# The M blocks of a feed-forward stage in the free columns of its two product banks, with a new order of that stage

## The chip, the cores and the metric

The kernel runs on one core of a Trainium2 chip. Its time is the device time of one execution in microseconds (us). TensorE (PE in the profile; PEld is its weight load), VectorE (DVE), ScalarE (ACT), GpSimd (POOL) and SyncE (SP, which issues the DMAs here) each work through a queue of their own in order, and wait for each other through semaphores.

## The reference, cut to what matters

```python
def reference(q, k, v, phi, w1, w2, w_in, w_out):
    x = attention(q, k, v)           # 4 x 8 heads, 576 positions, windowed -> 2304 x 512
    logits = x @ phi                 # 32 slots
    d = softmax over tokens (logits)
    slot_input = d.T @ x             # 32 x 512, four slots for each of 8 experts
    for e in range(8):
        slot_out[e] = relu(slot_input[e] @ w1[e]) @ w2[e]
    c = softmax over slots (logits)
    x = c @ slot_out                 # 2304 x 512
    h = x @ w_in                     # the feed-forward stage: 2304 x 2048
    return (relu(h) ** 2) @ w_out    # 2304 x 512
```

## The kernel before, in words

Attention, slots and experts come first, up to about 159 us. The change is in the last stage, the feed-forward.

The stage doesn't build `x`. Since x @ w_in = c @ (slot_out @ w_in), it first makes M = slot_out @ w_in, 32 rows, in ten **M blocks** `M0` to `M9` (four of 128 columns, six of 256; `CHUNKS`), each as soon as its weights are there. A block has three parts (`m_ops`): `M4.0` is the product on TensorE into a tile `pm` in PSUM, `M4.1` a rounded copy of it into `M3` in SBUF (tile `M`, on ACT or DVE), `M4.2` the rest of the rounding, taken as a difference by DVE (L953), which reads `pm` too. The other operand is `C3`, the transposed `c`, rounded and split in the same way: eight blocks of it are transposed by TensorE into tiles `c3p` (token `cp`), copied by ACT (`ca`) and finished by DVE (`cv`). Blocks 0 to 3 are the first half `C3a`, 4 to 7 the second `C3b`.

Then 96 **steps** follow. A step is one group of 384 tokens and one block of 128 hidden columns: `h` is the product of `C3` and `M3` into a PSUM tile `ph`, `u` its relu by ACT, `q` the rounded square (tile `hi`, on ACT or DVE), `g` the exact square, `l` their difference (tile `lo`, DVE), `oa` six matmuls of 512 columns with `hi` into the sums `acc`, `ob` three more with `lo`. `e` takes a finished sum out of `acc`.

The weights come as 64-bit floats and are converted on the chip: tokens `i4.0` to `i4.4` for block 4 of w_in, `o4.0` to `o4.4` for w_out (`.0` and `.1` on ACT or DVE, `.2` to `.4` on DVE), and `s4.0`, `s4.1` split w_out into two rounded tiles `wohl`. `.4` frees the slot of a ring of five, and the next load goes there.

What sets the order is the table `SEQ`: every token is one operation, and each engine gets its own in the order of the table. `SEGS` says which token groups (pairs of 384) run through which hidden blocks after each other: pair 0 with blocks 0 to 3, pair 1 with all 16, pair 0 with the rest, pair 2 with all. A pair that is left unfinished is parked in SBUF (`part`, `slotD`) and added back later.

Of the eight PSUM banks, six hold `acc`, and two are a pool `h` with two buffers, from which `ph`, `pm` and, from the fifth block on, `c3p` take a buffer in the order in which they are asked for. A buffer comes free when all readers of its tile have run.

Of the kernel before, what the change touches and what calls it, by code (L numbers as in the profile page):

```python
# [67 lines left out]
i4.3V i5.0A oa u o4.2V u ob q.V g.A q.V g.A h oa l u o5.1A l q.V ob g.V o5.0A i4.4V h oa e.A e.A e.V u ob l i6.1A q.V
h oa e.V e.A e.V g.A u ob o4.3V q.A h oa g.A l u l q.A g.V ob o6.1A o4.4V h oa u l s4.0A q.V ob g.V s4.1V h oa u q.A l
g.A i5.2V ob l h oa i5.3V u i7.1A q.V ob g.A i5.4V h oa u l q.A g.V ob o5.2V l M4.0 o5.3V oa M4.1A i6.0V M4.2V o6.0A  # L70
ob o5.4V h o7.1A h oa i6.2V u s5.0V u ob q.V g.A q.A g.V h oa u l l q.A g.A s5.1V ob h oa l u i6.3V i8.1A ob q.A g.V
M5.0 i6.4V oa l M5.1A o6.2V i7.0A M5.2V ob o6.3V o7.0A h h oa i7.2V u u o6.4V q.A ob g.A h q.V g.A oa l s6.0A l i7.3V
u ob o8.1A h oa s6.1V q.A g.A i7.4V u ob q.A M6.0 g.A l i9.1A l oa o7.2V M6.1A o7.3V i8.0A ob M6.2V oa o8.0A o7.4V h h
i8.2V s7.0A ob i8.3V M7.0 u u q.V g.A h cp q.V g.A oa l M7.1A l u s7.1V ca.A ob q.A g.A h M7.2V oa i9.0A l i8.4V u ob
o9.1A h q.V oa g.A o8.2V u l o9.0A ob q.V g.V h oa o8.3V u q.A g.A l ob o8.4V h oa u l s8.0A q.V ob g.V s8.1V h oa u
q.A l g.A cv ob l M8.0 i9.2V i9.3V oa M8.1A o9.2V ob M8.2V i9.4V cp h h ca.A oa u o9.3V u q.A ob g.A cv q.A g.V h oa l
u l q.A o9.4V g.A ob h l oa s9.0A u s9.1V ob q.A g.A M9.0 l oa M9.1A M9.2V ob h h oa u u q.V g.A q.V g.A ob l l h oa u
q.A g.V l ob h oa u q.A g.V l ob h oa u q.A g.V l ob h oa e.A e.V e.A u ob q.A g.V h l oa e.A e.V e.A u ob q.A g.V h l
oa u q.A g.V l ob h oa u q.A g.V l ob h oa u q.A g.V l ob h oa u q.A g.V l ob h oa u q.A g.V l ob h oa u q.A g.V l ob
h oa u q.A g.V l ob h oa u q.A g.V l ob h oa u q.A g.V l ob h oa u q.A g.V l ob h oa u q.A g.V l ob h oa u q.A g.V l  # L80
ob h oa u q.A g.V l ob h oa u q.A g.V l ob h oa u q.A g.V l ob h oa u q.A g.V l ob h oa u q.A g.V l ob h oa u q.A g.V
l ob h oa u q.A g.V l ob h oa u q.A g.V l ob h oa u q.A g.V l ob h oa u q.A g.V l ob h oa e.V u e.V q.A g.A e.V ob l h
# [1084 lines left out]
```

## Time and profile before

| | us |
|---|---|
| median of 3 runs | 407.81 (407.49 to 410.29) |
| the profiled execution's own time | 407.48 |
| its span, first to last instruction | 405.7 |
| TensorE busy | 388.1 (96%) |
| VectorE busy | 271.4 (67%) |
| ScalarE busy | 250.3 (62%) |
| GpSimd busy | 81.8 (20%) |

The busy times are means over stages with different limits. What a part of the stage is worth is seen where engines stand idle, and in what ends that.

### The profile page before, as it was taken

Reading aid. Unit: us, or ns where it says so; the run is one execution under the profiler, and the core shown is the slowest. Engines: PE = TensorE matmul, PEld = TensorE weight load, DVE = VectorE, ACT = ScalarE, POOL = GpSimd, SP = SyncE. Lnnn points to the kernel's source line nnn. Section 1 sums busy time; section 2 is a strip of 40 time slices with the busy share of each in tenths; the row PEclk is TensorE's granted clock in tenths of the full one; section 3 lists DMA queues with packets and bytes.
Section 4 is the critical chain, followed back from the end, with each engine's and each line's share of the span. In section 5 each row is a group of like instructions: output and inputs, shape, how many; then the busy total and the mean of one; then the engine's idle time right before and its main releaser. Section 6 shows DMA issues by size and latency. Waiting matters only on the chain.

```text
span 405.7 us, 8004 instructions
## 1 busy us (share of the span) xinstructions
PE 388.1 (96%) x2874; PEld 296.9 (73%) x2874; DVE 271.4 (67%) x624; ACT 250.3 (62%) x744; POOL 81.8 (20%) x167
## 2 busy tenths in 40 slices
PE   6899999999999998799999889999999999999996
PEld 3787887888874333578877677788888888888885
DVE  2699888788753227699999989665454565444452
ACT  4588888888853114699778974665444454444442
POOL 2677775757611002000000000000000000000000
PEclk9699999999999999699999999999999999999999
DMA  7998599999989999844454400003000040000004
GB/s 214 415 418 306 166 303 294 319 307 299 320 309 342 389 387 378 331 132 142 145 205 134 180 0 0 2 13 145 0 0 2 0 155 2 1 2 1 0 2 155
DMA packets 31992, 70.11 MB, mean 173 GB/s; under 512 B 2257, under 2 KB 5329, under 8 KB 31953
## 3 DMA queue, kind: packets, MB, share of 16 engines
q1 hardware_dynamic: 31952, 69.61, 48.7%
q8 instruction: 23, 0.38, 0.4%
q14 instruction: 17, 0.13, 0.1%
HBM read 64.88 MB, written 4.72 MB: 172 GB/s over the span
## 4 chain that ended last, share of the span: by engine, by line
PE 71%; DVE 12%; DMA 7%; ACT 5%; issue 3%; SPq 1%; POOL 0%; ACTq 0%; POOLq 0%; DVEq 0%
PE acc L1003 26%; PE acc L1009 13%; PE s L323 6%; PE o L372 5%; DMA slotC<-in_w_dram 4%; PE ph L975 4%; PE pt L358 3%; PE psh L759 3%; PE xnp L409 3%; DVE slotA L842 2%; PE s L320 2%; PE pacc L428 2%; DMA slotC<-in_kq_dram 2%; DVE cv L847 2%; DVE lo L997 2%
## 5 line engine op out<-in xcount | busy, mean ns | idle before, releaser
L1003 PE MATMUL acc<-wohl,hi 128*128 128x512 f32 x580 | 153.8, 398 | 1.0 <-ACT hi L990 1.0
L1003 PEld LDWEIGHTS acc<-wohl,hi 128*128 128x128 f32 x580 | 108.1, 190 | 24.2 <-ACT hi L990 1.6
L982 ACT ACTIVATE u<-ph 128x384 f32<-128x384 f32 x96 | 46.5, 490 | 76.4 <-PE ph L975 74.0
L1009 PE MATMUL acc<-wohl,lo 128*128 128x512 f32 x290 | 85.2, 396 | 0.0
L992 DVE TENSOR_TENSOR g<-u 128x384 f32<-128x384 f32 x66 | 36.9, 558 | 54.9 <-ACT u L982 54.9
L1009 PEld LDWEIGHTS acc<-wohl,lo 128*128 128x128 f32 x290 | 54.8, 189 | 13.0
L997 DVE TENSOR_TENSOR lo<-g,hi 128x384 fp32r<-128x384 f32 x96 | 52.8, 556 | 10.9 <-ACT g L990 3.2
L343 ACT ACTIVATE p<-s,ns 128x96 f32<-128x96 f32 x144 | 47.4, 343 | 6.7 <-DVE ns L337 6.3
L990 ACT ACTIVATE hi<-u 128x384 fp32r<-128x384 f32 x80 | 42.0, 526 | 2.2
L352 POOL TENSOR_TENSOR p<-p,ns 128x288 f32<-128x288 f32 x48 | 32.1, 671 | 27.2 <-DVE ns L351 14.1
L343 ACT ACTIVATION_READ_ACCUMULATOR p<-s,ns 128x1 f32 x144 | 29.7, 206 | 0.0
L337 DVE TENSOR_REDUCE ns<-s 128x3 f32<-128x288 f32 x48 | 21.7, 451 | 10.7 <-PE s L323 10.2
L713 POOL COPY c3n<-c_all 96x96 f32<-96x96 f32 x24 | 6.9, 326 | 101.0 <-PE c3p L725 101.0
L358 PE MATMUL pt<-ident,p 128*96 128x128 f32 x144 | 24.9, 284 | 0.6 <-POOL p L352 0.6
L199 POOL TENSOR_TENSOR slotC<-slotC,zero 32x384 f32<-32x384 f32 (+1 forms) x27 | 20.0, 746 | 7.8 <-ACT qz L312 6.6
L323 PE MATMUL s<-slotC,qz 128*128 128x96 f32 x126 | 18.4, 286 | 2.4 <-DVE qz L310 2.4
L323 PEld LDWEIGHTS s<-slotC,qz 128*128 128x128 f32 x126 | 17.6, 208 | 4.1 <-issue 3.8
L842 DVE SCALAR_TENSOR_TENSOR slotA<-slotA 128x1024 int32<-128x1024 int32 (+1 forms) x18 | 18.9, 1048 | 0.5 <-ACT slotA L835 0.4
L835 ACT ACTIVATE slotA<-slotA 128x1024 int32<-128x1024 uint32 (+1 forms) x18 | 17.9, 1001 | 1.9 <-DMA slotA<-in_w_in_dram 1.7
L975 PE MATMUL ph<-C3a,M 96*128 96x384 f32 x48 | 17.1, 360 | 1.8 <-DVE M L953 0.9
L847 DVE CUSTOM_DVE_ANT_0 cv<-slotA,cv 128x2048 uint16<-128x2048 uint16 (+1 forms) x18 | 18.7, 1042 | 0.1
L358 PEld LDWEIGHTS pt<-ident,p 128*96 128x96 f32 x144 | 16.6, 136 | 2.4 <-issue 1.1
(180 smaller groups left out, 561.3 us busy)
## 6 DMA issues: line engine op xcount, KB each, us to landing
slotB<-in_w_dram SPq DMA_DIRECT2D x14, 1024.0 KB, 6.7
slotC<-in_w_dram SPq DMA_DIRECT2D x12, 1024.0 KB, 6.8
slotA<-in_w_in_dram SPq DMA_DIRECT2D x6, 1024.0 KB, 5.4
slotA<-in_w_out_dram SPq DMA_DIRECT2D x6, 1024.0 KB, 4.9
slotA<-in_w_dram SPq DMA_DIRECT2D x5, 1024.0 KB, 6.3
slotC<-in_kq_dram SPq DMA_DIRECT2D x6, 576.0 KB, 8.1
slotB<-in_kq_dram SPq DMA_DIRECT2D x6, 576.0 KB, 7.7
out_dram<-e SPq DMA_DIRECT2D x11, 256.0 KB, 2.0
```

Of the source, the lines that this page charges most:

```text
L323: nc.tensor.matmul(s[:, i, :], lhsT=qz[n % QZ_BUFS][:, i, :], rhs=qk_t[u][1][:, QB * blk:QB * blk + KB], start=False, stop=(i == 2),)
L343: nc.scalar.activation(p[:, i, :], s[:, i, :], AF.Exp, bias=ng[:, i:i + 1], scale=-1.0, accum_out=sm[:, i:i + 1])
L352: nc.gpsimd.tensor_tensor(p, p, rs.unsqueeze(2).to_broadcast([128, 3, KB]), op=ALU.mult)
L358: nc.tensor.transpose(pt[:, i, :], p[:, i, :], ident)
L842: nc.vector.scalar_tensor_tensor(w[:, :, 1], w[:, :, 1], -2 ** 31, w[:, :, 0], op0=ALU.bitwise_and, op1=ALU.bitwise_or)
L975: nc.tensor.matmul(t, lhsT=pools["M3"][:, 128 * fc:128 * fc + 128], rhs=C3[half][:, t0:t0 + GT], start=True, stop=True)
L982: nc.scalar.activation(r, u_t[k], AF.Relu)
L990: nc.scalar.activation(t, r, AF.Square)
L992: nc.vector.tensor_tensor(t, r, r, op=ALU.mult)
L997: nc.vector.tensor_tensor(lo, g_t.pop(k), hi_t[k], op=ALU.subtract)
L1003: nc.tensor.matmul(a[:, c], lhsT=hi_t[k][:, sl], rhs=w[:, c], start=first, stop=False)
L1009: nc.tensor.matmul(a[:, c], lhsT=lo_t[k][:, sl], rhs=wo_hl[fc][0][:, c], start=False, stop=last)
```

## The change

The two PSUM banks of the stage are now two tiles held for good. `ph` and `c3p` take them in turn (`h_bank`), in columns 0 to 383 (0 to 287 for `c3p`). `pm` no longer takes a turn: block m lies in columns 384 to 511 of bank m mod 2. In the built program instructions on the same bank still wait for each other when they are on different engines, whichever columns they touch.

The table `SEQ` is another one. All four `c3p` blocks that were left for this stage come at its start; before, two of them stood after 24 and 31 finished steps. `M5` comes after 16 steps (18 before); `M4`, `M6`, `M7`, `M8` and `M9` come after 14, 22, 24, 30 and 34 in both. `SEGS` puts pair 2 before the rest of pair 0, so that the last six sums are now added to parked ones by DVE, where before they were copied by ACT and DVE. Some tokens have changed their engine: up to `M9.2`, `q` is 24 times on ACT and 12 times on DVE (22 and 14 before), `g` 23 and 13 (26 and 10 before).

```diff
-SEGS = [(0, 0, 4), (1, 0, 16), (0, 4, 16), (2, 0, 16)]
+SEGS = [(0, 0, 4), (1, 0, 16), (2, 0, 16), (0, 4, 16)]
...
-sel.A w2 P2 cp i1.0V i1.1A i1.2V i1.3V o1.1A M0.0 o1.0V i2.1A i1.4V i2.0A M0.1V M1.0 o2.1A o1.2V M0.2V o2.0A o1.3V h h
+sel.A w2 P2 cp i1.0V i1.1A i1.2V i1.3V ca.A M0.0 o1.1A cv o1.0A i1.4V cp M0.1A o1.2V i2.0A M1.0 M0.2V ca.A o1.3V i2.1A
...
@@ c3_pe
         if "h" in pools:
-            p = pools["h"].tile([96, 3, 96], F32, tag="h", name="c3p")
+            p = h_bank()[:96, :288].rearrange("p (j t) -> p j t", j=3)
@@ phase2
-        pools["h"] = ctx.enter_context(tc.tile_pool(name="pm_h", bufs=2, space=PSUM))
+        hp = ctx.enter_context(tc.tile_pool(name="pm_h", bufs=1, space=PSUM))
+        pools["h"] = [hp.tile([128, 512], F32, name=f"ph{i}") for i in range(2)]
+
+    def h_bank():
+        return pools["h"][nxt("hb") % 2]
@@ m_ops
-            t = box["t"] = pools["h"].tile([128, 128], F32, tag="h", name="pm")
+            t = box["t"] = pools["h"][nxt("mb") % 2][:, GT:GT + 128]
@@ st_h
-        t = u_t[k] = pools["h"].tile([128, GT], F32, tag="h", name="ph")
+        t = u_t[k] = h_bank()[:, :GT]
```

TensorE at the start of the stage, before: the fifth `c3p`, then `M0` and `M1` (`pm`), two products `ph`, the first sums.

```order
L725 MATMUL c3p<-ident,c3n 96x96 x3
L930 MATMUL pm<-cv_2317,sT 96x128 x4
L930 MATMUL pm<-cv,sT 96x128 x4
L975 MATMUL ph<-C3a,M_2591 128x384 x2
L1003 MATMUL acc<-wohl_2558,hi_2647 128x512 x6
L975 MATMUL ph<-C3a,M_2591 128x384
```

The same place now. `ph_2598` and `ph_2599` are the two banks; a row that reads `c3n` is a `c3p` block, one that reads `cv` an M block, one that reads `C3a` a product.

```order
L725 MATMUL ph_2598<-ident,c3n 96x96 x3
L934 MATMUL ph_2598<-cv_2317,sT 96x128 x4
L725 MATMUL ph_2599<-ident,c3n 96x96 x3
L934 MATMUL ph_2599<-cv,sT 96x128 x4
L979 MATMUL ph_2598<-C3a,M_2591 128x384
L979 MATMUL ph_2599<-C3a,M_2591 128x384
L725 MATMUL ph_2598<-ident,c3n 96x96 x3
L1007 MATMUL acc<-wohl_2558,hi_2658 128x512 x6
L979 MATMUL ph_2599<-C3a,M_2591 128x384
L725 MATMUL ph_2598<-ident,c3n 96x96 x3
```

The sixth to eighth `c3p` have moved in here, each ahead of work of the steps.

TensorE around `M7`, before: the sums of step 23, `M7`, the product of step 26, the seventh `c3p`, the sums of step 24.

```order
L1009 MATMUL acc<-wohl_3075,lo_3252 128x512 x3
L930 MATMUL pm<-cv,sT 32x128 x8
L975 MATMUL ph<-C3a,M_2591 128x384
L725 MATMUL c3p<-ident,c3n 96x96 x3
L1003 MATMUL acc<-wohl_3205,hi_3306 128x512 x6
```

The same place now.

```order
L1013 MATMUL acc<-wohl_3060,lo_3225 128x512 x3
L934 MATMUL ph_2599<-cv,sT 32x128 x8
L979 MATMUL ph_2598<-C3a,M_2591 128x384
L1007 MATMUL acc<-wohl_3179,hi_3286 128x512 x6
L1013 MATMUL acc<-wohl_3179,lo_3301 128x512 x3
```

The `c3p` is gone from between the product and the sums.

ScalarE around `M5` now, with the engines that each waits for: the relu of step 16 (`u_3070`), that of step 17 (`u_3081`), the rounded square of step 16 (`hi_3083`).

```order
L862 CAST wohl_3060<-cv 128x1024 [waits DVE_49]
L835 ACTIVATE slotA_72<-slotA_72 128x1024 [waits DMAHW5_49]
L986 ACTIVATE u_3070<-ph_2598 128x384 [waits PE_49]
L986 ACTIVATE u_3081<-ph_2599 128x384 [waits PE_49,Activation_49]
L994 ACTIVATE hi_3083<-u_3070 128x384 [waits Activation_49]
```

The relu of step 17 reads the bank `ph_2599`, into which `M5` is written before it; the semaphore value it waits for is that of `M5`'s last matmul.

## Rows read from the trace of the kernel before

**Rows 1.** Stretches: PE, PEld, DVE, ACT, POOL busy (x), PEclk, DMA share, GB/s.

```profile
159.50:165.40 5.90, 2.63 (x19) 1.95 (x17) 4.62 (x11) 4.04 (x8) 1.15 (x3) 0.99 1.06 384
165.40:172.00 6.60, 5.30 (x12) 4.03 (x13) 4.33 (x8) 4.36 (x10) 0.00 (x0) 0.50 0.85 323
178.00:231.50 53.50, 52.78 (x269) 42.06 (x268) 52.82 (x82) 46.66 (x84) 1.47 (x3) 1.00 0.47 159
235.00:251.40 16.40, 16.40 (x84) 13.11 (x83) 14.47 (x24) 10.91 (x21) 0.65 (x3) 1.00 0.00 0
260.90:402.10 141.20, 141.16 (x624) 115.68 (x624) 72.36 (x130) 66.08 (x134) 0.00 (x0) 1.00 0.08 30
```

**Rows 2.** The chain that ended last: a step, `M9`, the sums of step 34.

```profile
236.95 0.18 PE ph L975
237.13 1.40 PE acc L1003 x6
238.53 0.70 PE acc L1009 x3
...
259.88 1.00 PE pm L930 x16
260.87 1.60 PE acc L1003 x6
```

**Rows 3.** PE in order of time, the stage's start.

```profile
159.49 1.09 PE L930 MATMUL pm<-cv,sT 128*96 128x128 f32 x8
162.71 1.11 PE L930 MATMUL pm<-cv,sT 128*96 128x128 f32 x8 [2.13 <-DVE M L953]
...
167.39 2.93 PE L1003 MATMUL acc<-wohl,hi 128*128 128x512 f32 x6 [0.99 <-ACT hi L990]
...
170.43 1.48 PE L1009 MATMUL acc<-wohl,lo 128*128 128x512 f32 x3
```

**Rows 4.** ACT in order of time: the fifth `c3p` copied; the row ahead of step 24's relu.

```profile
172.88 0.38 ACT L736 CAST C3b<-c3p 96x288 fp32r<-96x288 f32 x1
...
229.95 1.06 ACT L862 CAST wohl<-cv 128x1024 fp32r<-128x1024 f32 x1
```

**Rows 5.** PE in order of time around the seventh and the last `c3p`.

```profile
231.57 1.07 PE L930 MATMUL pm<-cv,sT 128*32 128x128 f32 x16 [0.79 <-ACT u L982]
...
234.40 0.42 PE L725 MATMUL c3p<-ident,c3n 96*96 96x96 f32 x3 [1.39 <-ACT u L982]
234.61 1.64 PE L1003 MATMUL acc<-wohl,hi 128*128 128x512 f32 x6
...
252.76 0.45 PE L975 MATMUL ph<-C3b,M 96*128 96x384 f32 x1 [0.67 <-ACT u L982]
```

**Rows 6.** Stretches of DVE alone, from its first conversion for `M1`.

```profile
158.73:182.80 24.07, 19.58 (x41) 0.86 0.70 255
182.80:232.03 49.23, 48.71 (x74) 1.00 0.48 164
```

**Rows 7.** DVE in order of time: the rounded squares of steps 24 and 25.

```profile
231.56 1.02 DVE L992 TENSOR_TENSOR hi<-u 128x384 fp32r<-128x384 f32 x2
```

**Rows 8.** Groups of DVE by line and shape, from 159 to 262.

```profile
L847 DVE CUSTOM_DVE_ANT_0 cv<-slotA,cv 128x1024 uint16<-128x1024 uint16 x6 | 4.1, 684 | 0.0
...
L741 DVE TENSOR_TENSOR C3b<-c3p,C3b 32x288 fp32r<-32x288 f32 x4 | 1.8, 455 | 0.1
```

**Rows 9.** Groups of ACT by line and shape, from 159 to 262.

```profile
L835 ACT ACTIVATE slotA<-slotA 128x512 int32<-128x512 uint32 x6 | 4.0, 677 | 0.4 <-DMA slotA<-in_w_in_dram 0.3
...
L946 ACT CAST M<-pm 32x128 fp32r<-32x128 f32 x24 | 6.1, 255 | 5.5 <-PE pm L930 5.2
L736 ACT CAST C3b<-c3p 96x288 fp32r<-96x288 f32 x4 | 1.6, 393 | 2.1 <-PE c3p L725 2.1
```

**Rows 10.** The last copies on ACT, in order of time.

```profile
402.10 0.65 ACT L1073 COPY e<-acc 128x256 f32<-128x256 f32 x2 [2.21 <-PE acc L1009]
```

**Rows 11.** The line of the adds of parked sums (durations ns min/median/max).

```profile
L1071 DVE TENSOR_TENSOR slotD<-acc,slotD x4: 681/682/684, 326.8 to 329.4; 128x512 f32<-128x512 f32 x4
```

More of the change, by code (lines that the diff above doesn't have):

```diff
@@ L63 @@
 o0.0A x x x x i0.4V x t.A o0.1A x cp ca.A cv x x o0.2V cp ca.A cv x o0.3V so.AV x x P1 so.A o0.4V s0.0V s0.1V sel.V
-sel.A w2 P2 cp i1.0V i1.1A i1.2V i1.3V o1.1A M0.0 o1.0V i2.1A i1.4V i2.0A M0.1V M1.0 o2.1A o1.2V M0.2V o2.0A o1.3V h h
-M1.1A i2.2V u o1.4V u q.A M1.2V s1.0A g.V oa i2.3V q.A g.A s1.1V i3.0A h l u i2.4V ob i3.1A l q.A h oa o2.2V g.A o2.3V
-u ca.A l q.A ob o2.4V g.A i3.2V M2.0 o3.1A s2.0V o3.0A i3.3V oa M2.1A s2.1V i4.1A M2.2V i3.4V h i4.0A ob l h cv oa u
-o3.2V u o3.3V q.A g.A q.V ob g.A o3.4V M3.0 o4.1A l s3.0V cp o4.0A l oa s3.1V M3.1A i4.2V ca.A i5.1A ob M3.2V cv h h
@@ L68 @@
[L68 to L82, printed above, removed]
@@ L83 @@
-oa e.V u e.V q.A g.A e.V ob l h oa u q.A g.V l ob h oa u q.A g.V l ob h oa u q.A g.V l ob h oa u q.A g.V l ob h oa u
+sel.A w2 P2 cp i1.0V i1.1A i1.2V i1.3V ca.A M0.0 o1.1A cv o1.0A i1.4V cp M0.1A o1.2V i2.0A M1.0 M0.2V ca.A o1.3V i2.1A
+h cv M1.1A u M1.2V h o2.1A o1.4V cp q.A g.V ca.A oa s1.0V u cv o2.0A s1.1V q.A h l g.A cp i2.2V u ob i2.3V ca.A q.A h
+cv oa g.A i2.4V i3.1A l i3.0A M2.0 o2.2V u o2.3V o3.1A ob l M2.1A q.A o2.4V oa g.A M2.2V s2.0A i3.2V i3.3V o3.0A h ob
+s2.1V i4.1A h i3.4V oa u l u o3.2V q.A o3.3V ob g.A q.V g.A M3.0 o3.4V i4.0A l oa M3.1V s3.0A l o4.1A M3.2V ob s3.1V
@@ new lines @@
+o4.0A h i4.2V h oa i4.3V u u q.A g.V ob q.A g.V h i5.1A oa l l u i4.4V i5.0A ob h q.V oa e.A e.V e.A g.V u o4.2V ob
+o5.1A l h oa e.V e.A e.A q.V g.A o4.3V ob u o5.0A h oa l q.V g.A o4.4V u ob i6.1A h l oa q.A g.V u s4.0V o6.1A ob l
+q.V h g.A oa s4.1V u q.A l g.A ob i5.2V h i7.1A oa l i5.3V u ob q.A g.V i5.4V h oa u q.A l g.A ob o5.2V l M4.0 o5.3V
+oa M4.1A i6.0V o5.4V o6.0A ob M4.2V oa s5.0A i6.2V o7.1A s5.1V h h ob u i6.3V M5.0 u q.A g.A q.V h g.A oa l M5.1A l u
+i6.4V i7.0A ob h M5.2V oa q.A g.V u o7.0A o6.2V ob l q.A g.V h oa i8.1A o6.3V u ob l q.A g.V h o8.1A oa o6.4V u l ob
@@ new lines @@
+s6.0A q.V h g.V oa u s6.1V q.A g.A ob l l h oa i7.2V u i7.3V q.A g.A ob i9.1A l M6.0 i7.4V oa o7.2V M6.1A o7.3V i8.0A
+ob M6.2V o8.0A oa o7.4V h i8.2V h s7.0A ob i8.3V M7.0 u u q.V g.A h q.V g.A oa l M7.1A l u M7.2V i9.0A ob s7.1V h oa
+q.A g.A i8.4V u o9.1A ob l h oa q.V g.A o8.2V u o9.0A l ob q.V g.A o8.3V h oa u q.A l g.A o8.4V ob h oa l u s8.0A
+i9.2V q.V ob g.A s8.1V h oa u l q.A g.V ob i9.3V M8.0 l i9.4V oa M8.1A M8.2V ob o9.2V h o9.3V h oa u u q.A g.V q.A ob
+g.V l h oa l u o9.4V q.A g.A ob s9.0V h oa l u s9.1V q.A g.A ob l M9.0 oa M9.1A M9.2V ob h h oa u u q.V g.A q.V g.A ob
@@ L84 @@
+l l h oa u q.A g.V l ob h oa u q.A g.V l ob h oa u q.A g.V l ob h oa e.A e.V e.A u ob q.A g.V h l oa e.A e.V e.A u ob
+q.A g.V h l oa u q.A g.V l ob h oa u q.A g.V l ob h oa u q.A g.V l ob h oa u q.A g.V l ob h oa u q.A g.V l ob h oa u
 q.A g.V l ob h oa u q.A g.V l ob h oa u q.A g.V l ob h oa u q.A g.V l ob h oa u q.A g.V l ob h oa u q.A g.V l ob h oa
@@ L87 @@
 h oa u q.A g.V l ob h oa u q.A g.V l ob h oa u q.A g.V l ob h oa u q.A g.V l ob h oa u q.A g.V l ob h oa u q.A g.V l
-ob h oa u q.A g.V l ob oa e.A e.V e.A ob oa ob e.A e.V e.A
+ob h oa u q.A g.V l ob h oa e.A e.V e.A u ob q.A g.V h l oa e.A e.V e.A u ob q.A g.V h l oa u q.A g.V l ob h oa u q.A
+g.V l ob h oa u q.A g.V l ob h oa u q.A g.V l ob h oa u q.A g.V l ob h oa u q.A g.V l ob h oa u q.A g.V l ob h oa u
+q.A g.V l ob h oa u q.A g.V l ob h oa u q.A g.V l ob h oa u q.A g.V l ob h oa u q.A g.V l ob h oa u q.A g.V l ob h oa
+u q.A g.V l ob h oa u q.A g.V l ob h oa u q.A g.V l ob h oa u q.A g.V l ob h oa u q.A g.V l ob h oa u q.A g.V l ob h
+oa u q.A g.V l ob h oa u q.A g.V l ob oa e.V e.V ob e.V oa ob e.V e.V e.V
 """
```

## The prediction

> **What bounds the kernel now.** I read the stretches first [rows 1]. In the feed-forward stage TensorE is full wherever nothing goes wrong: busy 141.16 of 141.20 us after the last M block, and 52.78 of 53.50 us from 178.0 to 231.5. There no order of other engines can help; what can be won lies in the start of the stage (2.63 of 5.90 us, then 5.30 of 6.60 at a granted clock of 0.50, the 1.2 GHz level) and in a few waits later.
>
> The chain of waits then gives the price of work that can't go away [rows 2]: a step is 0.18 + 1.40 + 0.70 = 2.28 us on TensorE, a long M block 1.0 (1.1 with the gap ahead of it). From M9's end on the chain is steps alone; the sums of step 34 start at 260.87. So the question is only how much earlier they start.
>
> TensorE in order of time shows what ends each idle stretch. At the start [rows 3] M1 stands 2.13 us for the last reader of M0, and the first sums start at 167.39. That M1 waits for M0 with two buffers there means that the other one was held, and ACT shows by what: the fifth `c3p`, transposed at the stage's start, is copied at 172.88 only [rows 4]. Around M7 [rows 5] M7 stands 0.79 us for a relu, and the seventh `c3p` 1.39 us for another, since M7 has one buffer and the product of step 26 the other; the sums of step 24 start behind it at 234.61. The last `c3p` brings a wait of 0.67 us at 252.76.
>
> The other limit is DVE. From 182.80 to 232.03, the end of the rounded square of step 24 (the first of two from 231.56 on [rows 7]), it is busy 48.71 of 49.23 us [rows 6]. Up to there it has as much to do as the time holds, except at the start, where it idles 24.07 - 19.58 = 4.5 us.
>
> **The change part by part.** *The start.* I follow the new order with durations of rows. The fifth `c3p` and M0 now share a bank, so M0 waits until ACT has copied the `c3p`. ACT does that behind one conversion, which in the trace begins at 159.3: 159.3 + 0.68 + 0.39 = 160.3 [rows 9], against 159.49 before [rows 3]. This loses 0.8 us. M1 no longer waits for M0's reader: it needs its converted weights, which DVE finishes behind the `c3p` subtraction that M0's end (161.4) releases: 161.4 + 0.46 + 0.68 = 162.5 [rows 8], against 162.71. The first product needs M0 alone and follows M1 at 163.7. ACT reaches its relu behind a `c3p` copy (0.39), a conversion (0.68) and M1's copy (0.26), near 165.0, ends it at 165.4, has one more conversion ahead of the rounded square and ends that near 166.4. So the first sums start at about 166.4, 1.0 us before 167.39. They took 2.93 us for six matmuls at the low clock, in place of 1.40 [rows 2, 3]; I keep that, and should the clock not fall, TensorE would wait for DVE's differences instead.
>
> Then DVE decides. Up to the square of step 24 its work is the same within 0.2 us: two more `c3p` subtractions (2 x 0.46) and one more square (0.55 by the duration of rows 7 halved), against one short row less in each of three groups, one of them a copy of a finished sum. What changes is its idle time at the start. I find six waits there: for the first conversion on ACT (0.4), M0's end (0.7), a copy of `c3p` twice (0.3 and 0.65), M1's copy (0.35), M3's product (0.55), and some 0.35 in gaps: 3.3 us. Before it was 4.5. So M3 is done some 1.9 us earlier than 182.80 (0.7 of that is work which the new order does later, and which has to be paid by step 24), and TensorE is then ahead of DVE's work.
>
> *Around M7.* The `c3p` and its wait are gone, and M7 waits for no relu. TensorE could start the sums of step 24 at 229.1: those of step 5 at 181.8 (M3 done at 180.9, then two products and the rest of step 4), nineteen steps (43.3), four M blocks at 1.0. ACT's row ahead of step 24's relu waits for DVE as it did before [rows 4]. DVE ends the square of step 24 at 232.03 - 1.2 = 230.8, so the sums start at 230.9 in place of 234.61: 3.7 us. Here DVE is the bound, and what TensorE has won before is cover: the wait in front of M0, and a new one at M5. There the relu of step 17 reads M5's bank and waits for M5's end; behind it in ACT's queue stands the rounded square of step 16, which the sums behind M5 need: 0.39 for the relu, 0.42 for the square, less what the product between takes, 0.7 us. TensorE has 1.8 us in hand by then, so the 0.7 costs nothing unless DVE comes earlier than I think; then it is paid in full.
>
> *From step 24 to 34.* Before, 260.87 - 234.61 = 26.26 us. Ten steps and M8, M9 with their gaps are 22.8 + 2.1 = 24.9. The last `c3p` and its 0.67 us wait leave: 1.3 us gained. DVE had 1.9 us to spare from 235.0 to 251.4 (14.47 of 16.40) [rows 1], and keeps up.
>
> *The end.* The last two halves of a sum were copied by ACT, 0.65 us for both [rows 10]; now DVE adds them to a parked one. An add of 512 columns takes 0.68 us [rows 11], so two halves take 0.68 or, with a fixed cost in each, up to 0.8: I take 0.1 us lost. Between the first and last piece the new place of pair 2 changes nothing on TensorE: the same 96 steps, the same six sums in flight.
>
> *DMAs.* The converted blocks free the ring's slots some 1 to 4 us earlier, so loads are issued earlier by as much; ACT's first conversion of a block stands about as far behind them as before. I cost this at nothing, with the earlier issue as its cover; if a load is late, ACT waits, as it does now for 0.3 us in one row's group [rows 9].
>
> **A rule against the change.** The rows show M1 waiting 2.13 us for a reader of another tile [rows 3]; none shows two engines at once on different columns of one bank. The Trainium skill (PSUM — Partial Sum Buffer, "PSUM bank collisions raise a hardware error") says that different engines may not touch one bank in the same partitions at once, whichever columns, and that waits go by bank. No run here shows a collision; the order of the changed kernel has such waits (M5's relu). If columns alone decided, M0 would start 0.8 us sooner, the first sums as well, and the sum would be 401.8; by the rule the columns themselves are worth nothing, which is what I have used.
>
> **The sum.** 3.7 + 1.3 - 0.1 = 4.9 us. The profiled execution took 407.48 us, 0.3 under the median of 407.81, so I forecast 402.6.
>
> Bounds: if DVE loses as much at the start as before (4.5), the sums of step 24 start at 232.1 and the gain is 2.5 + 1.3 - 0.1 = 3.7: 403.8; if in addition the 1.3 doesn't come, 405.1. If DVE idles so little that TensorE is the bound, they start at 229.1, and the gain is 5.5 + 1.3 - 0.1 = 6.7: 400.8, or 400.1 if M5's wait goes too.
>
> **The rivals.** *DVE loses the same time elsewhere* (403.8 to 405.1). For it: DVE is busy 98.9% from 182.80 to 232.03, and each of the six waits at the start is a chain over three engines. Against it: before, DVE waited there for relus whose products themselves shared the one bank left free [rows 3, 4]. Chance 0.22.
>
> *The shared bank costs more than it frees* (slower). The place is the first product after an M block in the block's bank: it waits for four ACT copies (4 x 0.26) and DVE's two subtractions (0.6), in all some 1.9 us behind the block. TensorE has at least one step's sums (2.1) between the two in the new order. If DVE's queue puts its two rows off, each of six M blocks costs what is over the 2.1, up to the whole 1.9 if nothing else can run, and the relu held behind M5 delays all that ACT has queued. Six times 1.9 is 11.4; less the 4.9 gained that is 414. It decides from 0.8 us per block (4.9 / 6), that is when DVE's subtractions end more than 2.9 us behind a block's product. Chance 0.05.
>
> *The order is worth nothing*: banks still wait by bank, M0 starts later, and the time stays at 407.5. Against it is that the waits of 0.79, 1.39 and 0.67 us have their `c3p` taken away. Chance 0.06.
>
> **How the numbers follow.** The forecast (400.1 to 403.7) has 0.67. A change under 1% (4.1 us) can't be told from none here. DVE's rival and the third lie within 1% for nearly all of their chance; so faster by over 1% is 0.67, within 1% 0.28, slower 0.05. The range runs from the lower bound, 400.1, to 405.6, half a us above the bound in which neither term comes fully; this leaves out the slower rival, the third, and some 0.08 at the low end, where the clock might not fall at the start and DVE find its work sooner.
>
> **What would show it.** Right: the first sums near 166.4; no `c3p` behind 172 us; the sums of step 24 at 230.9 with their wait ended by DVE; step 34's at 255.7; DVE idle some 3.3 us up to M3. Wrong: TensorE waiting for DVE's or ACT's readers of M blocks; ACT waiting for a DMA; sums of step 24 behind 232.5; or, on the good side, no wait at step 24 at all.

## The result, and the profile after

The changed kernel takes 402.62 us (median of 4 runs, 401.85 to 403.1) where the kernel before took 407.65 beside it: a ratio of 0.9864, 95% interval 0.9816 to 0.9911. Run again later, the same kernel took 403.48 us beside 407.07. The profiled execution took 401.85 us with a span of 400.1; before, 407.48 and 405.7.

Stretches by engine say more than the two spans, because executions of one kernel begin the stage at different times. I cut at four rows that every version has: **S**, DVE's first conversion for `M1` (158.73 before, 157.20 after); the start of `M3`; the sums of step 24; the start of `M9`. The last three are rows of TensorE. Each line gives from:to, its length, then the busy time of PE, PEld, DVE, ACT and POOL with the number of instructions, the granted clock, the DMA share and GB/s. Before:

```profile
158.73:180.15 21.42, 16.50 (x74) 12.92 (x73) 16.96 (x36) 16.55 (x34) 1.15 (x3) 0.84 0.72 270
180.15:234.61 54.46, 52.28 (x281) 41.55 (x279) 53.91 (x83) 47.52 (x87) 1.47 (x3) 1.00 0.46 155
234.61:259.80 25.19, 24.52 (x121) 19.34 (x119) 22.37 (x35) 17.26 (x34) 0.69 (x3) 1.00 0.00 1
```

After:

```profile
157.20:176.79 19.59, 16.09 (x84) 13.08 (x82) 17.21 (x36) 16.59 (x37) 3.61 (x9) 0.91 0.82 296
176.79:230.02 53.23, 52.10 (x274) 41.10 (x272) 51.57 (x80) 46.76 (x82) 0.00 (x0) 1.00 0.47 159
230.02:254.12 24.10, 24.10 (x115) 19.05 (x116) 23.80 (x37) 17.23 (x38) 0.00 (x0) 1.00 0.00 1
```

From S to `M9` the stage is 4.15 us shorter (101.07 to 96.92): 1.83, 1.23 and 1.09. From `M9` to the end it takes 145.95 in place of 145.90, so the new last pieces cost 0.05. The other 1.53 us between the two profiled executions lies ahead of S, in instructions that the change leaves alone; the granted clock of the first 50 us was 0.93 before and 0.97 after.

TensorE after, in order of time, with what ended each idle stretch; these answer to [rows 3] and [rows 5]. In this kernel a `ph` that reads `cv` is an M block.

```profile
158.71 1.11 PE L934 MATMUL ph<-cv,sT 128*96 128x128 f32 x8 [0.66 <-ACT C3b L736]
...
161.15 1.11 PE L934 MATMUL ph<-cv,sT 128*96 128x128 f32 x8 [1.08 <-DVE cv L847]
162.02 0.42 PE L979 MATMUL ph<-C3a,M 96*128 96x384 f32 x1
163.85 0.44 PE L979 MATMUL ph<-C3a,M 96*128 96x384 f32 x1 [1.41 <-DVE M L957]
...
164.90 2.35 PE L1007 MATMUL acc<-wohl,hi 128*128 128x512 f32 x6 [0.36 <-ACT hi L994]
...
208.63 1.67 PE L1007 MATMUL acc<-wohl,hi 128*128 128x512 f32 x6 [0.69 <-ACT hi L994]
...
229.41 0.44 PE L979 MATMUL ph<-C3a,M 96*128 96x384 f32 x1 [0.27 <-ACT u L986]
230.02 1.67 PE L1007 MATMUL acc<-wohl,hi 128*128 128x512 f32 x6 [0.17 <-DVE hi L996]
```

The waits of 0.79, 1.39 and 0.67 us are gone, and `M1` stands 1.08 us for its converted weights in place of 2.13 for a reader of `M0`. New are 0.66 in front of `M0`, 1.41 in front of the second product and 0.69 in front of the sums of step 16. The sums of step 24 now start right behind DVE's square, and no `c3p` is left there: the last stands at 167.37.

ACT and DVE after around 197 us, in order of time. ACT stands for a load and does a relu behind it:

```profile
196.87 1.18 ACT L835 ACTIVATE slotA<-slotA 128x1024 int32<-128x1024 uint32 x1 [1.43 <-DMA slotA<-in_w_in_dram]
197.90 0.51 ACT L986 ACTIVATE u<-ph 128x384 f32<-128x384 f32 x1
```

DVE waits for that relu; further down stands its square of step 24:

```profile
198.44 0.56 DVE L996 TENSOR_TENSOR g<-u 128x384 f32<-128x384 f32 x1 [0.75 <-ACT u L986]
...
229.42 1.02 DVE L996 TENSOR_TENSOR hi<-u 128x384 fp32r<-128x384 f32 x2
```

This I had not expected. The last row holds the squares of steps 24 and 25; the first of them, half of it, ends near 229.9.

DVE alone, from S to the end of its last row for `M3`, and from there to the start of that square; the first line answers to the first of [rows 6]:

```profile
157.20:178.92 21.72, 19.14 (x40) 0.92 0.76 271
178.92:229.42 50.50, 49.05 (x74) 1.00 0.49 165
```

### The profile page after: what moved, and what is told of

Its sections match the earlier page's. It is cut to its first block, busy times and chain, and to the rows that moved or that the text cites. A ratio compares the mean times of both kernels' runs of the same rounds, so it can differ in the third digit from the quotient of the medians.

```text
span 400.1 us, 8014 instructions
## 1 busy us (share of the span) xinstructions
PE 386.1 (96%) x2874; PEld 295.6 (74%) x2874; DVE 272.8 (68%) x626; ACT 248.7 (62%) x742; POOL 82.1 (21%) x167
## 4 chain that ended last, share of the span: by engine, by line
PE 81%; DVE 6%; DMA 4%; ACT 3%; SPq 2%; issue 2%; POOL 0%; DVEq 0%; POOLq 0%; ACTq 0%
PE acc L1007 31%; PE acc L1013 16%; PE s L323 6%; PE o L372 5%; PE ph L979 4%; PE pt L358 4%; PE psh L759 4%; PE xnp L409 3%; DMA slotA<-in_w_in_dram 2%; PE s L320 2%; PE ph L934 2%; PE pacc L428 2%; DMA slotC<-in_kq_dram 1%; PE psl L443 1%; SPq L231 1%
## 5 line engine op out<-in xcount | busy, mean ns | idle before, releaser
L996 DVE TENSOR_TENSOR g<-u 128x384 f32<-128x384 f32 x71 | 39.5, 558 | 56.2 <-ACT u L986 56.0
L994 ACT ACTIVATE hi<-u 128x384 fp32r<-128x384 f32 x82 | 43.0, 527 | 2.2
L323 PEld LDWEIGHTS s<-slotC,qz 128*128 128x128 f32 x126 | 17.1, 203 | 3.1 <-issue 3.0
L323 PE MATMUL s<-slotC,qz 128*128 128x96 f32 x126 | 17.8, 280 | 1.5 <-DVE qz L310 1.5
L320 PE MATMUL s<-cb 128*128 128x288 bf16 x48 | 14.4, 301 | 2.0 <-ACT p L343 1.9
```

Of the source, the lines that this page charges most:

```text
L320: nc.tensor.matmul(s, lhsT=identb, rhs=mb[:, o:o + 3, :], start=True, stop=False)
L323: nc.tensor.matmul(s[:, i, :], lhsT=qz[n % QZ_BUFS][:, i, :], rhs=qk_t[u][1][:, QB * blk:QB * blk + KB], start=False, stop=(i == 2),)
L994: nc.scalar.activation(t, r, AF.Square)
L996: nc.vector.tensor_tensor(t, r, r, op=ALU.mult)
```

## The experiments

My theory at the outset: DVE sets the start of the sums of step 24, and what TensorE waits before them is cover, that is, time that costs nothing because DVE would have been waited for in any case. The rivals were that TensorE's waits add up, and that the columns, the new places of the `c3p` blocks, or the order as a whole each carry the gain. All times in this table are differences of the start times of the four rows named above, each from one profiled execution; the clock is the one granted from S to `M3`. The column DVE has, on DVE's own rows, the time from the end of its last row for `M3` to the start of its rounded square of step 24: where DVE sets the pace, an edit between the two is priced there, since TensorE's start of `M3` can come sooner without DVE being any further.

| kernel | S to M3 | clock | M3 to step 24 | DVE | step 24 to M9 | S to M9 | median us |
|---|---|---|---|---|---|---|---|
| before | 21.42 | 0.84 | 54.46 | 48.76 | 25.19 | 101.07 | 406.8 to 407.65 |
| changed | 19.59 | 0.91 | 53.23 | 50.50 | 24.10 | 96.92 | 402.62 |
| changed, again | 19.82 | 0.91 | 53.23 | 50.47 | 24.12 | 97.17 | 403.48 |
| order alone | 18.70 | 0.91 | 54.56 | 50.67 | 23.91 | 97.17 | 403.54 |
| fifth c3p early | 20.32 | 0.83 | 54.86 | 48.97 | 25.16 | 100.34 | 406.96 |
| late c3p early | 21.10 | 0.84 | 55.55 | 51.61 | 23.91 | 100.56 | 406.15 |
| both moved | 20.20 | 0.83 | 55.39 | 51.28 | 23.91 | 99.50 | 405.46 |
| relus ahead of M5 | 19.35 | 0.91 | 53.07 | 49.86 | 24.11 | 96.53 | 402.33 |
| two moves | 19.59 | 0.91 | 52.45 | 49.70 | 24.11 | 96.15 | 401.38 |
| DVE more, early | 18.65 | 1.00 | 54.43 | 51.14 | 24.09 | 97.17 | 403.51 |
| DVE more, late | 20.54 | 0.83 | 53.12 | 50.37 | 24.12 | 97.78 | 402.60 |
| other bank | 17.97 | 1.00 | 54.03 | 50.69 | 24.28 | 96.28 | 402.53 |
| DVE less | 20.59 | 0.83 | 52.55 | 49.81 | 24.11 | 97.25 | 402.42 |
| two moves, other bank | 17.97 | 1.00 | 52.74 | 49.43 | 24.28 | 94.99 | 400.32 |

**The order alone.** The new table and the new order of pieces in the old pool, with its whole-bank tiles; nothing else.

```diff
-SEGS = [(0, 0, 4), (1, 0, 16), (0, 4, 16), (2, 0, 16)]
+SEGS = [(0, 0, 4), (1, 0, 16), (2, 0, 16), (0, 4, 16)]
...
-sel.A w2 P2 cp i1.0V i1.1A i1.2V i1.3V o1.1A M0.0 o1.0V i2.1A i1.4V i2.0A M0.1V M1.0 o2.1A o1.2V M0.2V o2.0A o1.3V h h
+sel.A w2 P2 cp i1.0V i1.1A i1.2V i1.3V ca.A M0.0 o1.1A cv o1.0A i1.4V cp M0.1A o1.2V i2.0A M1.0 M0.2V ca.A o1.3V i2.1A
```

> The new table and the new sequence of pairs, with the old pool: an M block takes its turn in the two buffers again. I count from DVE's first conversion for M1 to the sums of step 24 and of step 34: 75.9 and 102.1 us in the kernel before, 72.8 and 97.9 in the changed one. My theory, that the order makes the gain (the fifth c3p copied at once, no c3p between later steps) and the columns nothing by themselves: 72.5 to 73.8 and 97.6 to 99.0, time within 1 us of the changed kernel's. The rival, that the M blocks' own columns make the gain: 75 and 101 or more, time at 406 to 408.

Measured: 403.54 us, ratio 0.9913 (0.9887 to 0.9939). TensorE of this kernel, in order of time:

```profile
162.56 1.11 PE L930 MATMUL pm<-cv,sT 128*96 128x128 f32 x8 [0.86 <-DVE M L953]
...
165.81 2.93 PE L1003 MATMUL acc<-wohl,hi 128*128 128x512 f32 x6 [0.46 <-ACT hi L990]
...
206.58 0.44 PE L975 MATMUL ph<-C3a,M 96*128 96x384 f32 x1 [0.66 <-DVE M L953]
208.91 1.07 PE L930 MATMUL pm<-cv,sT 128*32 128x128 f32 x16 [0.87 <-ACT u L982]
...
230.70 1.07 PE L930 MATMUL pm<-cv,sT 128*32 128x128 f32 x16 [1.10 <-ACT u L982]
```

Without the columns the waits of `M5` and `M7` for relus stay (0.87 and 1.10), with 0.66 ahead of `M5`. But `M0` waits for nothing, the first sums start 7.09 us after S in place of 7.70, and `M3` comes 0.9 sooner at the same clock. What the columns give from `M3` to step 24 (54.56 - 53.23 = 1.33) they take at the start (0.89) and behind step 24 (0.19): 0.25 us net in the first execution of the changed kernel, nothing in the second. The order carries the gain. Its DVE starts the square of step 24 71.99 us after S, in the changed kernel 72.22; what holds the sums of step 24 here is `M7`'s wait for a relu.

**The fifth c3p alone.** The kernel before, with that `c3p` copied right behind its transposes, so that both banks are free for `M0` and `M1`.

```diff
-sel.A w2 P2 cp i1.0V i1.1A i1.2V i1.3V o1.1A
+sel.A w2 P2 cp i1.0V i1.1A ca.A i1.2V i1.3V cv o1.1A
```

(The old `ca.A` and `cv` further down go.)

> The kernel before, with one thing moved: the fifth c3p block is copied by ACT and finished by DVE right behind its transposes, so its buffer comes free 12 us sooner. My theory, that this held buffer made the start slow: the wait of 2.13 us ahead of M1 goes, the first sums start 0.8 to 1.4 us sooner after DVE's first conversion (8.7 us before, 7.7 changed), the sums of step 24 about 1 us sooner, the waits at M7 stay or grow, time 0.5 to 1.3 us less. The rival, that the start is slow by the chain over ACT and DVE whatever the buffers: first sums at 8.4 to 8.8 us, time unchanged.

Measured: 406.96 us, ratio 0.9994 (0.997 to 1.0018). TensorE of this kernel, in order of time:

```profile
160.36 1.08 PE L930 MATMUL pm<-cv,sT 128*96 128x128 f32 x8 [1.92 <-DVE cv L847]
...
228.60 1.07 PE L930 MATMUL pm<-cv,sT 128*32 128x128 f32 x16 [0.90 <-ACT u L982]
231.43 0.42 PE L725 MATMUL c3p<-ident,c3n 96*96 96x96 f32 x3 [1.39 <-ACT u L982]
```

The bank is free, and `M1` waits 1.92 in place of 2.13: its weights come nearly as late as the bank did. The first sums gain 0.23 us relative to S (8.43 in place of 8.66), `M9` 0.73. My theory missed here; the rival, that the start is slow by the chain over ACT and DVE, had the numbers.

**The two late c3p blocks alone, and both edits together.** The seventh and eighth `cp ca cv` go from behind `M7` and `M8` to behind the relus of steps 11 and 13; then this together with the edit above.

```diff
-i8.2V s7.0A ob i8.3V M7.0 u u q.V g.A h cp q.V g.A oa l M7.1A l u s7.1V ca.A ob q.A g.A h M7.2V
+i8.2V s7.0A ob i8.3V M7.0 u u q.V g.A h q.V g.A oa l M7.1A l u s7.1V ob q.A g.A h M7.2V
...
-h oa g.A l u l q.A g.V ob o6.1A
+h oa g.A l u cp ca.A cv l q.A g.V ob o6.1A
```

> The kernel before, with the seventh and eighth c3p block moved from behind M7 and from step 31 to behind the relus of steps 11 and 13, where TensorE is full and DVE too. My theory: the waits of 1.39 and 0.67 us and the blocks' 0.2 us each leave their places; at step 24 DVE, which now has two more subtractions (0.9 us) ahead of it, decides: sums of step 24 at 74.2 to 74.8 us after DVE's first conversion (75.9 before), step 34 at 99.3 to 100.2 (102.1 before), time 1.9 to 2.8 us less. The rival, that those waits only stand where TensorE would have waited for DVE in any case: 75.6 to 76.8 and over 101.2, time less by under 0.9 us.

> The kernel before with both edits: the fifth block copied at once, and the seventh and eighth moved to behind the relus of steps 11 and 13. If the two are the cause and add up, sums of step 34 at 98.2 to 99.4 us after DVE's first conversion and time 2.7 to 4.1 us less than before, so the changed kernel's other reordering is worth little. If the new order as a whole is needed, 99.8 us or more and under 2.5 us less.

Measured: 406.15 us, 0.9981 (0.9957 to 1.0005); and 405.46, 0.9955 (0.9932 to 0.9977). The stretch from `M3` to step 24 with the late blocks moved:

```profile
178.92:234.47 55.55, 53.19 (x283) 41.77 (x282) 53.35 (x83) 46.57 (x85) 2.13 (x6) 1.00 0.47 152
```

Behind step 24 the 1.28 us come back (25.19 to 23.91), as predicted; ahead of it 1.09 are lost, so the forecast missed and the rival's numbers came (sums of step 24 at 76.65 after S, step 34 at 101.55). The work of the two blocks now stands in front of step 24, TensorE is busy 53.19 there in place of 52.28, and a product in that stretch waits 1.25 us for the second M reader (at 208.08). DVE stands 1.56 us there for the copy of the first moved block:

```profile
193.91 0.46 DVE L741 TENSOR_TENSOR C3b<-c3p,C3b 32x288 fp32r<-32x288 f32 x1 [1.56 <-ACT C3b L736]
```

Both edits together gain 1.57 us up to `M9`, the new order 3.90, in part with a higher clock at its start (0.91 against 0.83): moving the `c3p` blocks to these places is not what carries it. Other places in the old order were not tried.

**The relus ahead of M5.** The changed kernel, without the wait at step 16.

```diff
-oa M4.1A i6.0V o5.4V o6.0A ob M4.2V oa s5.0A i6.2V o7.1A s5.1V h h ob u i6.3V M5.0 u q.A g.A q.V h g.A
+oa M4.1A i6.0V o5.4V o6.0A ob M4.2V oa s5.0A i6.2V s5.1V h h ob u u q.A i6.3V M5.0 g.A q.V h o7.1A g.A
```

> The changed kernel with the relus of steps 16 and 17 and the rounded square of step 16 put ahead of M5 in the order, and one load moved behind the next product; the work is the same. It takes away the wait of 0.69 us that TensorE has at the sums of step 16. My theory (DVE sets the sums of step 24, and what TensorE waits before them is cover): the wait goes, the sums of step 24 stay within 0.3 us of 72.8 us after DVE's first conversion for M1, the start of M9 within 0.3 of 96.9 after it, and the time at 402.3 to 402.7. Rival (TensorE's waits add up): M9 0.7 us sooner, near 96.2, and the time near 401.9.

Measured: 402.33 us, ratio 0.9892 (0.9854 to 0.993). The wait of 0.69 is gone. `M9` starts 96.53 us after S, between the two forecasts. From `M3` to step 24 it takes 53.07 in place of 53.23, which looks like cover. But in this execution TensorE's start of `M3` stood 2.61 us ahead of DVE's last row for `M3`, in the changed kernel's 2.13. On DVE the same stretch is 0.64 us shorter:

```profile
177.57:227.43 49.86, 48.87 (x75) 1.00 0.49 168
```

The changed kernel's two executions and the one with more DVE work behind `M9`, all with the same instructions up to there, took 50.50, 50.47 and 50.37. In the changed kernel DVE, too, stands still behind `M5`, for ACT's exact square of step 16:

```profile
208.20 0.56 DVE L996 TENSOR_TENSOR hi<-u 128x384 fp32r<-128x384 f32 x1
209.02 1.03 DVE L1001 TENSOR_TENSOR lo<-g,hi 128x384 fp32r<-128x384 f32 x2 [0.26 <-ACT g L994]
```

With the edit it doesn't wait there, and 0.5 of the 0.64 comes at these two rows. So the wait at `M5` held DVE as well as TensorE, and most of it was paid; the rival is nearer to the mark than the theory. The edit also moves a conversion on ACT behind the relus, so the 0.5 can't be put down to the relus alone.

**Two moves.** Besides, the conversion that stood 1.43 us for its load goes behind the rounded square of its step.

```diff
-q.V h g.A oa s4.1V u q.A l g.A ob i5.2V h i7.1A oa l i5.3V u ob q.A g.V i5.4V
+q.V h g.A oa s4.1V u q.A l g.A ob i5.2V h oa l i5.3V u ob q.A i7.1A g.V i5.4V
```

> The edit of the run before, and besides the conversion of a slot on ACT that stood 1.43 us for its load near 197 us is put behind the rounded square of its step, so that ACT can do the relu that DVE waited 0.75 us for. My theory (DVE sets the sums of step 24, so what DVE idles ahead of them is lost in full): DVE's wait of 0.75 goes, the sums of step 24 come 0.5 to 0.8 us sooner (72.0 to 72.3 us after DVE's first conversion), M9 0.4 to 0.8 sooner, time near 401.9. Rival (the loads set the pace: the block of M5 is as late as its load, wherever its conversion stands): no change beyond the run before, or M5 itself later.

Measured: 401.38 us, ratio 0.9863 (0.983 to 0.9897).

```profile
174.91:227.36 52.45, 51.72 (x274) 41.09 (x273) 51.55 (x80) 46.45 (x82) 0.00 (x0) 1.00 0.49 161
```

DVE's wait of 0.75 is gone, and the sums of step 24 come 0.78 us sooner behind `M3` than in the changed kernel. Counted on DVE it is 0.80 (49.70), but only 0.16 less than with the first move alone. At the row that had stood for the relu DVE is 0.72 us further than there; then it waits 0.45 for another square of ACT, which has a conversion ahead of it:

```profile
206.83 0.56 DVE L1001 TENSOR_TENSOR lo<-g,hi 128x384 fp32r<-128x384 f32 x1 [0.45 <-ACT g L994]
```

So ACT's wait for a load, with a relu queued behind it, cost DVE 0.75 us; taking it away alone would not have been worth that much.

**More work for DVE, early and late.** Rounded squares of three steps on DVE in place of ACT: steps 13, 15 and 19, or steps 50, 54 and 58.

```diff
-q.V h g.A oa s4.1V u q.A l g.A ob i5.2V h i7.1A
+q.V h g.A oa s4.1V u q.V l g.A ob i5.2V h i7.1A
```

> The changed kernel with the rounded square of steps 13, 15 and 19 on DVE in place of ACT: DVE has 1.4 us more to do ahead of the sums of step 24, ACT 1.2 us less. My theory (DVE sets these sums): they start 1.1 to 1.4 us later (73.9 to 74.2 us after DVE's first conversion), M9 as much later (98.0 to 98.3), time near 403.9. Rival (ACT or TensorE sets them): the sums and the time stay, or come up to 1 us sooner, since ACT, whose queue holds the relus, has less to do.

> The same three squares' worth of work moved from ACT to DVE, but in steps 50, 54 and 58, behind the last M block, where TensorE is full. My theory: DVE has slack there, M9's start stays at 96.9 us after DVE's first conversion, and the stretch from M9 to the end stays at 146.0 us; time 402.4 to 402.8. Rival (any work more on DVE costs its own time): 1.4 us more in the last stretch, 404.0.

Measured: 403.51 us, 0.9917 (0.9889 to 0.9945); and 402.60, 0.989 (0.9857 to 0.9924). The early one, S to `M3` and `M3` to step 24:

```profile
156.81:175.46 18.65, 15.01 (x84) 12.11 (x84) 16.55 (x35) 16.34 (x37) 3.61 (x9) 1.00 0.85 305
175.46:229.89 54.43, 52.20 (x275) 41.03 (x273) 53.59 (x85) 45.74 (x79) 0.00 (x0) 1.00 0.47 157
```

The late one, S to `M3`:

```profile
158.42:178.96 20.54, 17.41 (x85) 14.15 (x85) 17.22 (x36) 16.72 (x37) 3.37 (x9) 0.83 0.79 286
```

With 1.4 us more DVE work ahead of step 24 the stretch from `M3` grows by 1.20; the same work behind `M9` costs nothing (145.97 us from `M9` to the end, 145.95 in the changed kernel). The 1.20 is too much for a price, since `M3` itself started 0.94 sooner in the early one, at a clock of 1.00. On DVE the stretch grows by 0.64:

```profile
178.14:229.28 51.14, 50.36 (x77) 1.00 0.49 163
```

DVE is busy 1.31 more in it and idles 0.78 in place of 1.45: half of the new work went into time in which it had waited. Both starts of `M9` missed what I had written, and for one reason: up to step 13 these two kernels and the changed one have the same instructions, yet S to `M3` took 18.65, 19.59 and 20.54 us, with the clock.

**The other bank.** Every M block in the other one of the two banks, same order.

```diff
-            t = box["t"] = pools["h"][nxt("mb") % 2][:, GT:GT + 128]
+            t = box["t"] = pools["h"][(nxt("mb") + 1) % 2][:, GT:GT + 128]
```

> The changed kernel with every M block in the other one of the two product banks; the order is the same. It asks what a shared bank costs, and whether waits go by bank. My theory (a wait is for the whole bank, whatever the columns): M0 no longer shares with the fifth c3p and starts 0.66 us sooner, 0.8 to 0.9 us after DVE's first conversion for M1 in place of 1.5; but M1 then shares with the first product, which waits 1 to 1.5 us for M1's readers, and the first sums, which need its relu, start 0.5 to 1.3 us later (8.2 to 9.0 us after that conversion). Further on DVE sets the pace: from M3 to the sums of step 24 53.0 to 53.6 us, as the 53.23 of the changed kernel. Time 403.2 to 404. Rival (columns alone decide): M0 and the first product start as in the changed kernel, and nothing changes: 402.6.

Measured: 402.53 us, ratio 0.9878 (0.982 to 0.9937). TensorE of this kernel, S at 158.78:

```profile
159.68 1.09 PE L934 MATMUL ph<-cv,sT 128*96 128x128 f32 x8
...
162.35 1.08 PE L934 MATMUL ph<-cv,sT 128*96 128x128 f32 x8 [0.73 <-DVE cv L847]
163.19 0.42 PE L979 MATMUL ph<-C3a,M 96*128 96x384 f32 x1
164.19 0.44 PE L979 MATMUL ph<-C3a,M 96*128 96x384 f32 x1 [0.58 <-DVE C3b L741]
...
165.46 1.67 PE L1007 MATMUL acc<-wohl,hi 128*128 128x512 f32 x6
...
207.92 1.07 PE L934 MATMUL ph<-cv,sT 128*32 128x128 f32 x16 [0.87 <-ACT u L986]
```

`M0` starts 0.90 us after S, as I expected. The first sums start 6.68 after S where I had written 8.2 to 9.0: the first product stands ahead of `M1`'s readers in the order, so it follows `M1` in the same bank at once, and the readers come behind it. At `M5` the wait moves from the sums to the block itself (0.87), and `M3` to step 24 grows to 54.03 (on DVE's rows by 0.19 only); I had not foreseen that either.

**Less work for DVE.** The two moves, and the plain squares of steps 14 and 21 on ACT.

```diff
-u ob q.A i7.1A g.V i5.4V h oa u q.A l g.A ob
+u ob q.A i7.1A g.A i5.4V h oa u q.A l g.A ob
...
-s6.0A q.V h g.V oa u s6.1V q.A g.A ob
+s6.0A q.V h g.A oa u s6.1V q.A g.A ob
```

> The two moves of before, and the differences' square rows of steps 14 and 21 (the second square of a step, unrounded) on ACT in place of DVE: 0.94 us less DVE work between M3 and the sums of step 24, and as much more for ACT in places where it idles. My theory (DVE sets the sums of step 24; behind it TensorE, which idles 0.73 us in the 52.45 from M3 to there): DVE's wait at the sums of step 24 goes, these come 0.3 to 0.7 us sooner (51.8 to 52.1 us after M3), the stretch from step 24 to M9 stays at 24.1, time near 400.9. Rival (ACT, which holds the relus, is as full as DVE): the wait is ended by ACT instead and nothing is won, or it is 0.3 us later.

Measured: 402.42 us, ratio 0.9877 (0.982 to 0.9934). `M3` to step 24:

```profile
178.36:230.91 52.55, 51.82 (x274) 41.08 (x272) 50.78 (x78) 47.08 (x84) 0.00 (x0) 1.00 0.48 161
```

and DVE in order of time near the end of that stretch:

```profile
219.38 1.22 DVE L867 TENSOR_TENSOR wohl<-cv,wohl 128x1024 fp32r<-128x1024 f32 x1 [0.32 <-ACT wohl L862]
```

The rival is right here: DVE's 0.77 us less work turn into idle time, and this row starts 41.02 us after `M3` where in the two moves it started 41.09 after (216.00). There it waits for ACT, and up to the square DVE takes 49.81 against 49.70. So "DVE sets step 24" holds up to the two moves; from there TensorE (51.82 busy of 52.55) and the waits of DVE for ACT leave less than a us for any one of them. With the M blocks in the other bank the two moves took 52.74, below.

**The changed kernel again, and the two moves in the other bank.**

> The changed kernel unaltered, beside the run after it and for one more execution of it. It asks how much of the start's length differs between executions of the same instructions. My theory: from M3 on every execution is the same, so M3 to the sums of step 24 takes 53.1 to 53.3 us and step 24 to M9 24.1; ahead of M3 the length follows the granted clock there: 18.6 us at 1.00, 19.3 to 19.6 at 0.91, 20.5 at 0.83. Time 402.3 to 403. Rival (the start is as long in every execution, and other runs differed by their edits): 19.6 us from DVE's first conversion for M1 to M3, whatever the clock.

> The changed kernel with the two moves of before (relus of steps 16 and 17 ahead of M5; the conversion that stood for a load behind its step's square) and every M block in the other product bank. My theory: M0 starts 0.9 us after DVE's first conversion for M1 and the first sums 6.5 to 6.9 after it, 0.8 to 1.2 sooner than in the changed kernel; the relu that M5 waits for in the other bank now stands ahead of it, so M5 waits at most 0.3; M3 to the sums of step 24 takes 52.4 to 52.8 us. M9 starts 94.9 to 96.0 us after the conversion (by the clock at the start) in place of 96.9; time 401.0 to 401.6. Rival (DVE has the same work up to step 24, and what M3 gains is lost ahead of it): M9 at 96.2, the time that the two moves alone give, 401.4 to 402.3.

Measured: 403.48 us (runs from 401.27 to 405.0), ratio 0.9888 (0.985 to 0.9925); and 400.32 (398.71 to 402.42), ratio 0.9822 (0.9786 to 0.9858). The second by stretches, S to `M3`, to step 24, to `M9`:

```profile
158.44:176.41 17.97, 15.31 (x85) 12.03 (x84) 16.58 (x35) 15.55 (x36) 3.55 (x9) 1.00 0.86 310
176.41:229.15 52.74, 51.88 (x275) 41.06 (x273) 52.19 (x82) 47.27 (x84) 0.00 (x0) 1.00 0.49 161
229.15:253.43 24.28, 24.28 (x116) 19.08 (x116) 23.44 (x36) 17.30 (x38) 0.00 (x0) 1.00 0.00 1
```

The changed kernel's `M3` to step 24 took 53.23 us to the hundredth again; its start was 19.82 at a clock of 0.91, 0.2 above what I gave. The other kernel has both gains, the early first sums (6.67 after S) and no relu to wait for at `M5`. On the same chip it is 3.2 us under the changed kernel, though the two intervals still touch (at 0.985 to 0.9858); from S to `M9` it is 2.18 shorter, in one execution each. It is the best version found. Whether whole-bank tiles would gain as much from the two moves was not run.

## Why the prediction was right, and where it was off

The time came out at 402.62 against 402.6. That is closer than the sum deserves: up to the end of the tail the change is worth 4.15 - 0.05 = 4.10 us in the profiled pair, not 4.9, part of that goes with a clock that the sum had left as it was ("DVE more, late", with the same instructions up to `M9`, was granted 0.83 at the start, about as the kernel before, and is 101.07 - 97.78 = 3.29 us shorter up to there), and the median pairs gave 5.03 and 3.59. With 3.6 to 5.0 between medians, a few tenths of agreement are luck.

- *The start.* `M0` lost 0.75 relative to S (0.8 predicted), `M1` came in at about the same place (3.95 and 3.98 after S), the first sums gained 0.96 (1.0). The chain over the three engines was read rightly up to there. DVE idled 2.58 us (21.72 - 19.14) up to its last row for `M3`, against 3.3 predicted and 4.5 before, and ended it 2.35 sooner (1.9). But a part of that is not the change's. `M3` started 1.83 sooner on TensorE; at the same clock, 0.83 to 0.84, the kernel before and its version with the late blocks moved took 21.42 and 21.10 up to there and this order 20.54 to 20.59, so 0.5 to 0.9 is the order's and about 1.0 goes with the clock in that execution. I had kept 2.93 us for the first six matmuls; they took between 1.67 and 2.93 by execution.
- *Around M7.* The prediction put the sums of step 24 right behind DVE's square (2.5 of the 3.7 us), and that came: 2.45. The other 1.2, DVE ending that square earlier, was the mis-sized term: it measured 0.6. It had assumed that DVE would lose nothing more behind `M3`. DVE's idle time up to `M3` fell by 1.9, not 1.2; but from there to the square it rose from 0.5 to 1.45, and DVE's work up to the square by 0.4 in place of at most 0.2: 1.9 - 0.9 - 0.4 = 0.6. The new idle time is 0.75 at 198 behind ACT's wait for a load, which I had costed at nothing ("DMAs"), and 0.26 behind `M5`. The text had named the first sign ("ACT waiting for a DMA"). So the first rival, DVE losing time elsewhere, came in part.
- *M5.* The wait of 0.7 came as 0.69, but it was not the cover that the prediction took it for: the relu that stands for `M5` holds ACT's squares, DVE waits for one of them, and DVE is the bound. With the order changed there, DVE reached the square of step 24 0.64 us sooner behind `M3`, 0.5 of it at `M5`.
- *From step 24 on.* 1.09 gained up to the sums of step 34 (255.12 - 230.02 is 25.10, against 260.80 - 234.61 = 26.19 in the same view; the 26.26 of the prediction takes 260.87 from the chain), 1.3 predicted; 0.05 lost from `M9` on, 0.1 predicted.
- *The bound.* That DVE sets step 24 is shown by the row (the sums wait for its square and start right behind it) and by more work for it (0.64 on DVE's rows for 1.4) beside the same work behind `M9` (nothing), within the limit found with less work.
- *The columns.* The prediction took them as worth nothing in themselves and the order as the gain; order alone against the changed kernel shows that, at the same clock: 0.0 to 0.25 us in single executions. The second rival (the shared bank costs more than it frees) had the right mechanism, waits of 0.66, 1.41 and 0.69 us, at a price that the freed waits paid back.

As for waits by whole banks, the rows show `M0` waiting 0.66 us for the copy of a `c3p` in other columns of its bank, and not waiting when it lies in the other bank. The Trainium skill (PSUM — Partial Sum Buffer, "PSUM bank collisions raise a hardware error") has waits added between engines that touch the same bank in the same quadrant of partitions, whatever the address there. This agrees with it, but what the run shows is a wait in the program, in which a bank is one tile, so that a wait by tile would look the same; none tried two engines at once in one bank.

## What to carry to other kernels

A buffer that is freed is worth what waits last behind it: the fifth `c3p`'s bank held `M1` for 2.13 us, and freeing it left 1.92 for the weights. Price an order as a whole, by the work and the waits of the engine that sets the pace, between two of its own rows: a wait that looks like cover on TensorE can stand in DVE's way through ACT. Look for rows where an engine stands for a load with another engine's input queued behind it. Sharing a bank has a parity: which bank a block lands in moved the first sums by 1.0 us, and decides which relu it waits for.
